# Six late heads of wo in place of four at the end of the load stream of a decode kernel

## The chip, the cores and the metric

One core of a Trainium2 chip. PE is its engine for matmuls (TensorE), DVE and ACT are the vector and the scalar engine, SyncE (SP in the views) issues the loads, and PSUM is the memory that the matmuls write. The granted clock is the share of PE's full clock that the records show. The time is that of one execution on the device, in microseconds, as a median over executions. The profiles are single executions; the span in a profile is shorter than the time of the same execution (652.63 against 654.05 for the kernel before), and a place in the trace counts from the start of the span.

## The reference

One decode step: attention of one query token over a KV cache of 8192 positions, then an output projection, gated by a small MLP. The cache is what costs: 4 batches x 8 KV heads x 8192 x 256 x 2 bytes, twice, is 268 MB of the 279 MB that the core reads.

```python
def _A_ref(x, k_cache, v_cache, wq, wo):      # x: (4, 1, 448), caches: (4, 8, 8192, 256)
    q = (x @ wq).reshape(B, Sq, 16, 256).transpose(0, 2, 1, 3)
    k, v = repeat(k_cache, 2, axis=1), repeat(v_cache, 2, axis=1)
    p = softmax(einsum("bhqd,bhkd->bhqk", q, k) * 256 ** -0.5)
    o = einsum("bhqk,bhkd->bhqd", p, v)
    return o.transpose(0, 2, 1, 3).reshape(B, Sq, 4096) @ wo     # wo: (4096, 448)

# xn = layernorm(x); the result is x + A(xn, ...) * silu(B(xn, ...)), B a small two-layer block
```

## The kernel before

There are 32 pairs of batch and KV head ("heads" 0 to 31 below). For each, PE transposes K by matmuls, DVE and ACT carry the transposes out of PSUM, PE makes the scores, and so on; V's product for a head is made while the next but one is at work. All large loads go through one queue, in the order in which SyncE issues them. The 16 query heads of `wo`, the weights of the output projection (229 KB each), are loaded in two parts: twelve at the front, behind the first two K loads, and four at the very end, behind the last pieces of V.

```python
    PIECES = (0, 32, 48, 56, NCH)          # the last V comes in four pieces
    LATE = ((0, 1), (2,), (3,))            # heads of wo that are loaded last: one load each group
    NLATE = sum(len(g) for g in LATE)
# ...
            load_k(0)
            load_k(1)
# ...
            load_wo(NLATE, HQ, "dwo")          # the early load of wo
            for h in range(2, NH):
                load_k(h)                      # waits until the K buffer of head h - 2 is free
                load_v(h - 2)                  # waits until the V buffer is free
            load_v(NH - 2)
            load_v(NH - 1)                     # four pieces
            for i, hs in enumerate(LATE):
                load_wo(hs[0], hs[-1] + 1, "dwl%d" % i)
```

After the last head, PE runs `finish`. It fills waits with products of heads of `wo` that are there already (`f_ou`) and with idle matmuls (`f_warm`), takes the last V piece by piece, and ends with the output products that need the late heads (`f_o`: four matmuls of 224 columns for a head).

```python
            def finish():
                f_bc(h)
                take(pe, "dwo", 16)
                f_ou(range(NLATE, HQ - 3 * REP))
                take(pe, "v_po")
                f_warm(4)
                take(pe, "a_exp")
                # ... four heads more of f_ou, products of V of head 30, then of the first pieces of 31
                f_direct(NPIECE - ND)
                take(pe, "v_po")
                # ... eight small matmuls (L775 of the profile)
                f_direct(NPIECE - 1).then_inc(S["p_pv"], 1)
                take(pe, "dwl0", 16)
                f_o(LATE[0])
                take(pe, "v_ot")
                f_o(range(HQ - REP, HQ))       # the two heads that need the last V
                for i in range(1, len(LATE)):
                    take(pe, "dwl%d" % i, 16)
                    ins = f_o(LATE[i], i == len(LATE) - 1)
                ins.then_inc(S["p_o"], 1)
```

DVE then multiplies by the gate and adds x, and the result is stored.

## Time and profile before

| | kernel before |
|---|---|
| time, median of 3 | 653.84 us (653.25 to 654.87) |
| bytes read, mean rate | 279 MB, 427 GB/s over the span |
| last K lands, first transpose of it | 617.39, 617.53 |
| last V piece lands, its first use | 646.59, 648.19 |
| last wo load lands | 648.82 |
| output matmuls | 648.79 to 650.31 |

From the page of the profile, the span in 40 slices: the clock that PE was granted in tenths, and the busy share of the 16 DMA engines in tenths; then the bytes read.

```profile
PEclk9977999898889987888888789988878997797989
DMA  9999999999999999999999999999999999999996
HBM read 278.99 MB, written 0.00 MB: 427 GB/s over the span
```

The load stream is full from the first slice to the last but one. A kernel like this can only end earlier if the stream ends earlier, or if less is left to do after it.

SyncE's issues at the end (start, duration, what), from the timeline of that engine, and for two of them the time from issue to landing from the view of the DMA issues:

```profile
590.31 0.33 SPq L251 DMA_DIRECT2D kn<-in_A_k_cache_dram  x1
616.47 1.85 SPq L266 DMA_DIRECT2D kn<-in_A_v_cache_dram  x4
620.60 8.43 SPq L276 DMA_DIRECT2D wo_sb<-in_A_wo_dram  x1
...
kn<-in_A_k_cache_dram SPq DMA_DIRECT2D x1, 4096.0 KB, 27.1
wo_sb<-in_A_wo_dram SPq DMA_DIRECT2D x1, 224.0 KB, 28.2
```

The last K was issued at 590.31 and landed 27.1 us later, at 617.4; the last wo load landed at 620.60 + 28.2 = 648.8. All landings in this text are read so, from the single issues.

PE at the end, from its timeline (start, duration, what):

```profile
646.72 0.57 PE L733 MATMUL pst<-pT,kn 128*128 128x32 bf16 x16
647.38 1.10 PE L775 MATMUL pst<-sel,po 128*128 128x32 f32 x8
648.31 0.56 PE L733 MATMUL pst<-pT,kn 128*128 128x32 bf16 x16
648.79 1.52 PE L723 MATMUL pst<-wo_sb,OT_all 128*32 128x224 bf16 x24
```

The 24 output matmuls are one row: no wait for a load inside. The last load landed at 648.82, when only the first two of them had started; the four that need it started at 649.9. The chain of work that ended last (start, duration, what) says the same, it goes back through PE's own work and not to a load:

```profile
647.38 1.10 PE pst L775 x8
648.47 0.39 PE pst L733 x16
648.87 1.46 PE pst L723 x24
650.33 0.02 issue
650.35 0.40 DVE res L559
```

And the clock in the last head: busy time by engine in one stretch (PE, PEld, DVE, ACT, POOL), then PE's granted clock, the DMA share and GB/s. Over most of this stretch the clock was halved; the records have it at half from 617.3 to 624.1.

```profile
617.00:624.50 7.50, 6.97 (x85) 6.79 (x86) 2.14 (x4) 3.16 (x7) 0.00 (x0) 0.54 0.99 428
```

### The profile page before, as it was taken

The page shows a single profiled execution, that of the slowest core. Times are in us where ns is not written, and L with a number is a line of the kernel's source. Part 1 is how long each engine was busy: PE and PEld are TensorE (multiplying, and loading weights), DVE is VectorE, ACT ScalarE, POOL GpSimd, SP SyncE. Part 2 cuts the span into 40 slices and gives each one's busy share as a digit, 9 for nine tenths or more (in the row PEclk, how much of TensorE's full clock was granted, in tenths as well). Part 3 has the DMA queues.
Part 4 walks back from the last instruction along what each step waited for, and adds up shares of the span by engine and source line. Part 5 has one row for each costly group of instructions (what it writes and reads, how often), then busy time and mean ns, then how long its engine had stood idle before and what let it go on. Part 6 is the DMA issues. An engine that isn't in the chain of part 4 may idle for free. (4 is left out here: it accounts for less than half of the span.)

```text
span 652.6 us, 22794 instructions
## 1 busy us (share of the span) xinstructions
PE 553.5 (85%) x9927; PEld 474.8 (73%) x9927; DVE 276.6 (42%) x622; ACT 256.2 (39%) x364; POOL 3.6 (1%) x17
## 2 busy tenths in 40 slices
PE   2889997987888988888998888898888898887898
PEld 1668886876667887766887676698767678775785
DVE  7433554443444443444444344444344444343442
ACT  3423553443324443433444233444333344342340
POOL 2000000000000000000000000000000000000000
PEclk9977999898889987888888789988878997797989
DMA  9999999999999999999999999999999999999996
GB/s 380 443 414 436 427 436 428 440 428 440 428 440 428 438 430 436 432 434 434 434 431 430 434 432 436 430 438 428 440 428 440 428 436 430 438 428 440 428 428 285
DMA packets 12497, 279.13 MB, mean 428 GB/s; under 512 B 1220, under 2 KB 3272, under 8 KB 3784
## 3 DMA queue, kind: packets, MB, share of 16 engines
q1 hardware_dynamic: 12472, 278.99, 99.4%
q8 instruction: 7, 0.11, 0.1%
q14 instruction: 2, 0.02, 0.0%
q10 hardware_dynamic: 16, 0.01, 0.0%
HBM read 278.99 MB, written 0.00 MB: 427 GB/s over the span
## 5 line engine op out<-in xcount | busy, mean ns | idle before, releaser
L624 PE MATMUL pst<-ident_b,kn 128*128 128x128 bf16 x4096 | 347.1, 239 | 78.2 <-PEq L294 77.1
L325 ACT ACTIVATE kT<-pst 128x1024 bf16<-128x1024 bf16 x224 | 229.5, 1025 | 359.3 <-ACTq L294 358.2
L624 PEld LDWEIGHTS pst<-ident_b,kn 128*128 128x128 bf16 x4096 | 276.0, 108 | 84.3 <-issue 83.7
L323 DVE COPY kT<-pst 128x1024 bf16<-128x1024 bf16 x288 | 197.6, 691 | 261.5 <-DVEq L294 261.5
L636 PE MATMUL psc<-qc,kT 128*128 128x2 bf16 x4096 | 178.3, 164 | 2.1 <-issue 2.1
L636 PEld LDWEIGHTS psc<-qc,kT 128*128 128x128 bf16 x4096 | 157.2, 98 | 31.4 <-issue 31.2
L675 PE MATMUL psv<-vb,pT 128*4 128x512 bf16 x1056 | 87.7, 384 | 0.0
L654 PE MATMUL psm<-sel,po 128*128 128x2 f32 x272 | 36.8, 257 | 0.5 <-PEq L294 0.5
L654 PEld LDWEIGHTS psm<-sel,po 128*128 128x128 f32 x272 | 34.8, 196 | 1.0 <-issue 1.0
L675 PEld LDWEIGHTS psv<-vb,pT 128*4 128x4 bf16 x1056 | 22.3, 82 | 14.9 <-issue 0.9
L483 DVE TENSOR_REDUCE rmax<-psc 128x2 f32<-128x128 f32 x32 | 9.3, 292 | 48.8 <-DVEq L294 48.8
L501 DVE COPY po<-psv 128x512 f32<-128x512 f32 x34 | 23.5, 691 | 3.0 <-DVEq L294 2.3
L488 DVE TENSOR_REDUCE gmax<-psm 2x1 f32<-2x128 f32 x32 | 8.9, 279 | 33.4 <-DVEq L294 33.4
L347 ACT ACTIVATE pT<-psc,negb 128x64 bf16<-128x64 f32 x66 | 20.7, 333 | 5.4 <-ACTq L294 5.4
L648 PEld LDWEIGHTS psm<-diag,ones_f 2*128 2x128 f32 x66 | 14.1, 264 | 6.4 <-issue 5.2
L648 PE MATMUL psm<-diag,ones_f 2*128 2x2 f32 x66 | 16.8, 322 | 1.0 <-PEq L294 0.9
L347 ACT ACTIVATION_READ_ACCUMULATOR pT<-psc,negb 128x1 f32 x66 | 13.6, 206 | 0.0
L644 PEld LDWEIGHTS psm<-ident_f,rmax 128*2 128x2 f32 x32 | 2.6, 80 | 14.4 <-issue 14.4
L666 PE MATMUL psm<-rowsum,ones_f 128*128 128x2 f32 x64 | 11.6, 251 | 0.0
L666 PEld LDWEIGHTS psm<-rowsum,ones_f 128*128 128x128 f32 x64 | 9.5, 188 | 0.0
L491 DVE TENSOR_SCALAR diag<-ident_f,gmax 2x2 f32<-2x2 f32 x32 | 6.9, 217 | 4.8 <-DVEq L294 1.4
L569 PE MATMUL pst<-ident_b,xn_b 4*128 4x4 bf16 x14 | 0.7, 163 | 9.6 <-DVE xn_b L395 9.6
(101 smaller groups left out, 98.7 us busy)
## 6 DMA issues: line engine op xcount, KB each, us to landing
kn<-in_A_k_cache_dram SPq DMA_DIRECT2D x31, 4096.0 KB, 25.5
vb<-in_A_v_cache_dram SPq DMA_DIRECT2D x31, 4096.0 KB, 31.1
kn<-in_A_k_cache_dram SPq DMA_DIRECT2D x2, 2048.0 KB, 24.6
vb<-in_A_wq_dram SPq DMA_DIRECT2D x1, 3584.0 KB, 11.1
vb<-in_B_w_dram SPq DMA_DIRECT2D x2, 1568.0 KB, 15.4
wo_sb<-in_A_wo_dram SPq DMA_DIRECT2D x1, 2688.0 KB, 42.5
kn<-in_A_v_cache_dram SPq DMA_DIRECT2D x1, 2048.0 KB, 25.1
kn<-in_A_v_cache_dram SPq DMA_DIRECT2D x1, 1024.0 KB, 27.1
```

The costliest lines, as they stand in the source:

```text
L323: engine.tensor_copy(dst, src).then_inc(S["v_ev"], 1)
L325: engine.activation(dst, src, ACT.Copy).then_inc(S["a_ev"], 1)
L347: ins = act.activation(pv_p[:, :, hh], sc[:, :, hh], ACT.Exp, bias=negb[:, s, hh:hh + 1], scale=SCALE, accum_out=rowsum[:, s, hh:hh + 1])
L483: v.tensor_reduce(rmax[:, :], psc[h % 2][:, 0:NCH * REP].rearrange("p (k h) -> p h k", h=REP), AX.X, ALU.max).then_inc(S["v_rmax"], 1)
L488: v.tensor_reduce(gmax[:, :], psm[0:REP, 0:P], AX.X, ALU.max).then_inc(S["v_s"], 1)
L501: v.tensor_copy(po[:, slot], psv[:, 0:CP * DH]).then_inc(S["v_po"], 1)
L624: ins = pe.transpose(dst[:, t * P:(t + 1) * P], kn[:, h % 2, GC * j + kl, half * P:(half + 1) * P], ident_b[:, :])
L636: ins = pe.matmul(psc[h % 2][:, kk * REP:(kk + 1) * REP], kT[:, j % RING, t * P:(t + 1) * P], qc[:, h % 2, half, :], start=(half == 0), st ...
L648: pe.matmul(psm[:, P:P + REP], ones_f[0:REP, :], diag[:, :], start=True, stop=True).then_inc(S["p_m2"], 1)
L654: ins = pe.matmul(dst(dh)[:, 0:width], po[:, slot, i * DH + dh:(i + 1) * DH:NHALF], sel[:, i, 0:width], start=(i == 0), stop=(i == CP - 1))
L666: pe.matmul(psm[:, P + REP:P + 2 * REP], ones_f[:, :], rowsum[:, h % 2, :], start=True, stop=True)
L675: ins = pe.matmul(psv[o:o + CP * REP, 0:CP * DH], pT[:, h % 2, kk * REP:(kk + CP) * REP], src[:, kk:kk + CP, :].rearrange("p c d -> p (c d)"),
```

## The change

The intent: two more heads of `wo` (459 KB) go from the early load to the end. All of K and V lands earlier by the time that those bytes take, and PE can finish the last head under the loads of `wo`. The late heads come in loads of two, two, one and one.

```diff
-    LATE = ((0, 1), (2,), (3,))
+    LATE = ((0, 1), (2, 3), (4,), (5,))
```

In the instruction order this takes four matmuls of 448 columns out of the first `f_ou` group (12 to 8) and adds eight of 224 columns to the last group (24 to 32). The early load has ten heads in place of twelve, and SyncE issues one load more. DVE, ACT and GpSimd are the same.

## The prediction

> **What bounds the kernel now.** Two things in turn. Almost everywhere it is the load stream: the 40-slice row shows the 16 DMA engines at nine tenths or more in every slice but the last, 428 GB/s over the span, 279 MB in one queue. No load is issued too late by the issue and landing times; tightest are the K load of head 3 (issued 61.28 us, the one before it landed 65.57) and that of head 2 (issued 40.18, the one before, wo, landed 46.23). PE waits for each K load: the last K (head 31) lands at 617.39 and its first transpose starts at 617.53.
>
> From there to the end it is no longer the stream but the chain of PE, DVE and ACT on the last head. Landings in the trace against use: V pieces land 641.62, 644.07, 645.35, 646.59 and are first used at 643.49, 645.12, 646.72, 648.19; late wo lands 647.70, 648.26, 648.82 and the 24 output matmuls run without a gap from 648.79 to 650.31. Every landing comes 1 to 2 us before its use. The chain of waits agrees: PE and DVE work, no DMA.
>
> **What the change does.** The bytes stay; two heads of wo (459 KB) move from the load behind the first two K loads to the end of the stream. The 12-head load took 6.66 us (39.57 to 46.23), so two heads take 1.11 us. Everything between, the last K and V pieces included, lands 1.11 us earlier; the last wo load still lands at about 648.8. One more DMA issue costs nothing: SP has 20 us to spare.
> PE: four matmuls of 128x448 leave the first group after the last head (about 0.75 us, but PE then waits for ACT's exponentials, so about 0.1 us of it counts), and eight of 32x224 join the last group, 55 ns apart by their starts: +0.44 us, on the critical path.
>
> **Sum.** -1.11 (last K earlier) +0.44 (eight more matmuls at the end) and 0 to -0.1 (shorter first group) = about -0.7 us on an execution like the profiled one. The last wo load would be used at about 649.4, still 0.6 us after landing.
>
> The gain depends on the state of the PE clock in the last head. In the profile the granted clock was half from 617.3 to 624.1 and that head took 17.3 us from first transpose to its row-maximum transpose; others took 14.6 with no half-clock stretch, 16.0 with 3.4 us of it. [...] its half-clock stretches are 3.4 or 6.8 us. So executions differ. Where the last head is fast, both kernels end on the last wo load at the same time and the gain is about zero. Average: -0.5 us.
>
> **Predicted time:** 653.3 us, range 652.4 to 654.1. Faster by over 2%: 0.5%; within 2%: 99%; slower by over 2%: 0.5%.
>
> **Right if:** the last K lands near 616.3, the last V piece near 645.5, the last wo load still near 648.8; 32 output matmuls end near 649.6 in one run without a gap; the chain of waits still ends in PE and DVE work.
>
> **Wrong if:** the shorter early wo load lets the queue run dry before the K load of head 2 or 3 (their margins fall to 5 and 3.2 us); small late loads run slower than 413 GB/s, so that a gap opens in the 32 matmuls; or the clock's phase hides a difference of 0.5 us.

## The result

653.59 us (653.26 to 654.64, 6 runs) against 653.56 (653.25 to 654.87, 6 runs). The ratio is 1.000, with a 95% interval of 0.9987 to 1.0013, that is 0.85 us either way.

The changed kernel's profile, in the same views. The slices and the bytes:

```profile
PEclk9997999897798979779987888998788988878999
DMA  9999999999999999999999999999999999999997
HBM read 278.99 MB, written 0.00 MB: 428 GB/s over the span
```

The issues at the end, and the time to landing of two:

```profile
591.90 0.33 SPq L251 DMA_DIRECT2D kn<-in_A_k_cache_dram  x1
614.77 1.85 SPq L266 DMA_DIRECT2D kn<-in_A_v_cache_dram  x4
634.76 3.60 SPq L276 DMA_DIRECT2D wo_sb<-in_A_wo_dram  x1
...
kn<-in_A_k_cache_dram SPq DMA_DIRECT2D x1, 4096.0 KB, 24.6
wo_sb<-in_A_wo_dram SPq DMA_DIRECT2D x1, 224.0 KB, 14.3
```

The last K landed at 616.48 (0.9 us earlier) and the last wo load at 649.04 (0.2 us later). PE's end:

```profile
645.92 0.56 PE L733 MATMUL pst<-pT,kn 128*128 128x32 bf16 x16
646.90 0.98 PE L723 MATMUL pst<-wo_sb,OT_all 128*32 128x224 bf16 x16 [0.43 <-PEq L294]
648.06 1.53 PE L723 MATMUL pst<-wo_sb,OT_all 128*32 128x224 bf16 x16 [0.17 <-PEq L294]
```

Now there are waits: before the first output matmul, between the two rows, and inside the second, where the starts of single matmuls jump from 648.78 to 649.18. Those are the landings of the four late loads (646.77, 647.92, 648.49, 649.04). The chain of work that ended last has no PE work left before the last four output matmuls:

```profile
649.18 0.42 PE pst L723 x4
649.60 0.02 issue
649.62 0.39 DVE res L559
650.02 0.02 issue
650.04 0.38 DVE out_b L561
```

So in this execution the last load decided the end, where in the profile before it was PE's chain. The clock differed as well: only 3.4 us at half in the last head.

```profile
617.00:624.50 7.50, 7.50 (x126) 7.38 (x123) 3.52 (x6) 4.68 (x8) 0.00 (x0) 0.77 1.01 437
```

The two profiles are thus one execution with a slow last head and one with a faster last head, and the time between the medians is nil. Two profiles can't tell whether the change or the clock made the difference.

### The profile page after: what moved, and what is told of

Its sections match the earlier page's. It is cut to its first block, busy times and chain, and to the rows that moved or that the text cites. A ratio compares the mean times of both kernels' runs of the same rounds, so it can differ in the third digit from the quotient of the medians.

```text
span 651.9 us, 22804 instructions
## 1 busy us (share of the span) xinstructions
PE 552.0 (85%) x9931; PEld 474.3 (73%) x9931; DVE 276.6 (42%) x622; ACT 256.0 (39%) x364; POOL 3.6 (1%) x17
## 5 line engine op out<-in xcount | busy, mean ns | idle before, releaser
L675 PE MATMUL psv<-vb,pT 128*4 128x512 bf16 x1056 | 86.1, 379 | 0.0
L648 PE MATMUL psm<-diag,ones_f 2*128 2x2 f32 x66 | 16.1, 310 | 1.1 <-PEq L294 0.9
L644 PEld LDWEIGHTS psm<-ident_f,rmax 128*2 128x2 f32 x32 | 2.6, 80 | 14.0 <-issue 14.0
```

Of the source, the lines that this page charges most:

```text
L648: pe.matmul(psm[:, P:P + REP], ones_f[0:REP, :], diag[:, :], start=True, stop=True).then_inc(S["p_m2"], 1)
L675: ins = pe.matmul(psv[o:o + CP * REP, 0:CP * DH], pT[:, h % 2, kk * REP:(kk + CP) * REP], src[:, kk:kk + CP, :].rearrange("p c d -> p (c d)"),
```

## The experiments

Theory A: the end is the later of two. One is the last wo load plus a fixed rest. The other is PE's chain, which starts when the last K lands and is longer when the clock is halved in the last head. The change moves the chain and not the last load, so it helps only executions in which the chain is the later one. Theory B: the chain gains in all executions, but the additional small loads end the stream later and take it back. Theory C: the shorter early load of `wo` gives it back, because the queue runs short before K of head 2 or 3, whose issue must wait for a buffer.

Twelve kernels ran, in three calls, each on one chip with its own runs of the kernel before: 653.77 us in the first call, 653.82 in the second, 653.50 in the third (medians of 11).

### Two late heads

```diff
-    LATE = ((0, 1), (2,), (3,))
+    LATE = ((0,), (1,))
```

> The opposite direction: two late heads (one and one) in place of four. Theory A (the kernel ends with the later of two things: the last wo load plus its few matmuls, or the PE chain that starts with the last K load): the last K lands 1.1 us later than in the kernel before, eight output matmuls fewer give 0.44 us back, so +0.2 us where the last head runs fast and +0.7 us where the clock is halved for long; median about 654.0 to 654.3, and in the profile the output matmuls follow the work before them without a gap while the last wo load has landed over 1 us before. Theory B (moving bytes to the end gains on the chain, but the extra small loads end the stream later and take it back): fewer late loads end the stream about 0.1 to 0.2 us earlier, time equal to the kernel before or lower.

654.86 us (654.13 to 655.42) against 653.77, ratio 1.0018 (1.0005 to 1.0031). The last K landed at 618.79, the last wo load at 649.09, where it is in the changed kernel too. So fewer late loads do not end the stream earlier, which speaks against theory B. The output matmuls ended at 650.37, 1.28 us after the last landing: chain-bound, although the last head was a faster one (16.0 us). The loss by the medians, 1.1 us, is above the 0.7 us that theory A gave at most, though the interval (0.3 to 2.0 us) includes that. In the profile the eight matmuls saved did not pay: from the last transpose of the last head's maxima to the end of the output matmuls it took 15.44 us, as in the kernel before. The longer first group took 0.20 us more, and with only four matmuls ahead of `v_ot`, PE's starts there were 0.38 us apart, against 0.19 before.

### Eight late heads

```diff
-    LATE = ((0, 1), (2,), (3,))
+    LATE = ((0, 1), (2, 3), (4, 5), (6,), (7,))
```

> Eight late heads (2, 2, 2, 1, 1). Theory A: the end is set by the last wo load, which lands at the same time as before within 0.2 us (648.8 to 649.1), so the time is that of four and of six late heads in a fast execution, about 653.3, and even the executions with the longest half-clock stretch no longer show, so that the spread shrinks to under 0.6 us. Gaps stand in the 40 output matmuls. Theory B: each further small load costs, so the last landing moves to 649.2 or later and the time goes up by 0.2 us or more against the changed kernel.

653.74 us (653.39 to 654.49) against 653.77, ratio 0.9998 (0.9985 to 1.0011). The end of PE, from its timeline:

```profile
646.98 2.44 PE L723 MATMUL pst<-wo_sb,OT_all 128*32 128x224 bf16 x36
649.58 0.41 PE L723 MATMUL pst<-wo_sb,OT_all 128*32 128x224 bf16 x4 [0.16 <-PEq L294]
```

The last four matmuls waited for the last load, although the clock was at half for 6.8 us in this last head and it took 17.3 us, as long as in the profile before. That is theory A: with eight late heads the slow clock no longer shows. But the spread did not shrink under 0.6 us as expected, and the last load landed at 649.44, 0.4 us late, as theory B had it. The place of the loss is not the end, though, and not the number of loads. From the last K to the last wo landing it took 30.29, 31.43, 32.57 and 33.69 us with two, four, six and eight late heads: 1.12 to 1.14 us for each two heads. With six heads in a single load (next experiment) it took 32.55 us, with six in four loads 32.57, so small loads cost the stream nothing that shows. The loss that the profile shows is at the front: the K loads of heads 2 and 3 took 10.15 and 10.10 us in place of 9.67. They were issued only 3.4 and 3.9 us before the load in front of them landed. That is what theory C expects, at a larger dose than in the change; but in two profiles below a load issued 4.0 us ahead lost nothing (9.67 us, the changed kernel with the fill) and one issued 4.6 us ahead lost 0.34 (10.01 us, the changed kernel again), so the lead alone does not decide it.

### Six late heads in one load

```diff
-    LATE = ((0, 1), (2,), (3,))
+    LATE = ((0, 1, 2, 3, 4, 5),)
-                f_o(range(HQ - REP, HQ))
+                ins = f_o(range(HQ - REP, HQ), len(LATE) == 1)
```

> Six late heads, but in one load, so that 24 of the 32 output matmuls have to wait for the last byte (the eight of the last pair of heads run before them or behind them). Theory A: +1.1 to +1.5 us against the changed kernel (20 to 28 more matmuls of 55 ns behind the last landing), about 654.7; this shows that the last landing is what the end hangs on. Theory B: three loads fewer, stream ends 0.2 us earlier or so, so +0.9 or less. If the time does not move, the last landing does not bound the end.

656.57 us (655.70 to 659.78), ratio to before 1.0047 (1.0028 to 1.0066): +2.8 us by the medians, twice the expectation. The direction is theory A's, the last landing (649.08) decides. In the profile 2.6 us of it lie between that landing and the end of the span (5.46 us, against 2.86 in the changed kernel), and 0.5 us outside the span, unexplained. Part of the 2.6 us has another cause, seen in PE's timeline and in the stretch of it:

```profile
649.22 3.00 PE L723 MATMUL pst<-wo_sb,OT_all 128*32 128x224 bf16 x32 [2.69 <-PEq L294]
...
649.20:652.30 3.10, 3.00 (x32) 2.79 (x32) 0.04 (x1) 0.00 (x0) 0.00 (x0) 0.57 0.00 0
```

PE stood still for 2.7 us before the load; in the records the clock was then halved from 648.5 to 651.9, and 32 matmuls took 3.0 us, 94 ns each, where 24 took 1.5 in the kernel before. So here loads in small steps were worth more than their matmuls: they also kept PE at work (in the profile of the changed kernel PE's longest wait there was 0.43 us, and the clock was full from 635 us on). The half-clock stretch lasted 3.4 us and began 1.9 us into the idle stretch of 2.7 us.

### Filling PE's wait for K

Twelve idle matmuls at the head of each head's work, in the kernel before and in the changed one.

```diff
+            def f_fill(h, n):
+                ptf = pT[:, :, :].rearrange("p s n -> p (s n)")
+                for i in range(n):
+                    pe.matmul(psc[h % 2][0:PVW, 0:ptf.shape[1]],
+                              pT[:, h % 2, NCH * REP:NCH * REP + PVW], ptf, start=True, stop=True)
             def body(h):
+                f_fill(h, 12)
```

> The kernel before with 12 idle matmuls (320 columns, about 0.14 us each, result overwritten) at the head of each head's work, where PE waits about 2 us for K. Theory A with the clock as the cause of the slow executions: the clock is no longer halved in the last head (granted clock near 1.0 over the span), that head takes about 14.6 us in place of 16 to 17.3, and all executions end on the last wo load, about 653.2, spread under 0.6 us; the kernel before gains 0.3 us and its slow executions (654.9) vanish. If the clock stays as it was, the cause of the spread is not shown by this run. If the clock is full and the spread stays, the clock was not its cause.

> The changed kernel with the same 12 idle matmuls at the head of each head's work as in the run with the kernel before (653.33 us there, span 651.9, last head 14.6 us). Theory A (later of last landing and PE chain; in fast executions the last landing decides in both kernels): 653.3 us, the same as the kernel before with the fill within 0.2 us, the output matmuls with gaps, last landing 649.0. Theory C (the shorter wo load at the front leaves the queue too little work, so that the K load of head 2 or 3 is issued late and starts with a loss): K of head 2 is issued under 3 us before the load in front of it lands, its own load takes 10.1 us or more in place of 9.67, everything after it lands later by as much, and the time is 653.7 or more.

Kernel before with fill: 653.33 us (653.24 to 653.94), ratio 0.9993 (0.9981 to 1.0006). Changed kernel with fill: 653.48 us (653.21 to 653.65), ratio 0.9991 (0.9978 to 1.0004). The last head took 14.59 us in both profiles. In the kernel before with fill, the stretch of the last head has the full clock, and PE's output matmuls now come 0.75 us sooner, behind a wait:

```profile
617.00:624.50 7.50, 6.75 (x132) 6.67 (x133) 3.52 (x6) 4.57 (x8) 0.00 (x0) 1.00 0.97 419
...
648.04 1.56 PE L731 MATMUL pst<-wo_sb,OT_all 128*32 128x224 bf16 x24 [0.42 <-PEq L294]
```

So the clock in the last head made the chain late, and without that the kernel before is bound by its last load too, as theory A says. Two marks of the expectation were missed: the mean clock was 0.958 and not near 1.0, and the spread 0.70 us in place of under 0.6. Theory C got little support at this dose: in the changed kernel with the fill, the K load of head 2 was issued 4.0 us ahead and took 9.67 us, as usual, and that of head 3, issued 5.0 us ahead, took 9.91, 0.24 us too long.

The fixed rest can be read from all profiles. From the landing of the last wo load to the end of the span it took 2.86 or 2.87 us in the changed kernel (two profiles), with eight late heads, in both filled kernels and in the kernel with an early load of only four heads further down, all with a wait before the last output matmuls. In the kernel before it took 3.81 us, with two late heads 3.59, with the front half of the change alone (two heads in mid-stream) 3.37, all without such a wait. That is the mark of the two regimes, where four matmuls follow the last load: 2.87 us is the floor, what is above it is the chain.

An estimate from these profiles tells where the two ends cross. In the kernel before, the first transpose starts 0.14 us after the last K, the last head follows, and then 15.44 us to the end of the output matmuls; by the other way the last load lands 31.43 us after the last K, and the four last matmuls end 0.55 us later. The two are equal for a last head of 16.4 us. In the changed kernel (32.57 us, and a chain 0.18 us longer, see below) it is 17.4 us. In the profiles of both kernels, heads with 3.4 us of half clock took 16.0 to 16.1 us, those with 6.5 or 6.6 us 17.3 to 17.4. So the kernel before is bound by its chain only when clearly more than 3.4 us of its last head run at half clock, and the changed kernel hardly ever. The same sum gives 0.73 and 0.51 us above the floor for the profiles with two late heads and with the front half alone; measured were 0.72 and 0.50.

### A longer chain, by PE

To see the chain's own gain in the time, 20 idle matmuls went into `finish` of both filled kernels.

```diff
                 f_ou(range(NLATE, HQ - 3 * REP))
+                f_warm(20)
```

> The kernel before with the fill and 20 idle matmuls (448 columns, about 3.7 us) in the PE chain right after the last head. Both kernels must now be bound by the chain and the clock is full, so that the chain's own gain is seen without the rest. Theory A: chain end of the filled kernel without stream waits 647.8 plus 3.6, so output matmuls end at about 651.4 in place of 649.6, time about 655.1. No gaps in the 24 output matmuls.

> The changed kernel with the fill and the same 20 idle matmuls. Theory A: 0.5 to 0.8 us faster than the kernel before with fill and delay (1.11 us from the earlier K load, 0.44 us given back by eight more output matmuls), about 654.4; no gaps in the 32 output matmuls or only at the last load. If the two are equal, the chain itself did not gain and theory A is wrong. If theory C holds too, the last K lands less than 1.11 us earlier.

660.45 us (660.14 to 661.02) and 657.14 us (656.45 to 659.93), ratios to before 1.0101 (1.0086 to 1.0116) and 1.0057 (1.0039 to 1.0075). That is 5.3 us and 2.7 us more than expected, so these times can't be used for the chain. The cause is in mid-kernel, where the outer loop begins its second round and the inner loop's code is needed again after a jump over the `finish` code. First, for the kernel before with fill and delay, the instruction packets on the page (number, MB, share) and PE's wait before the first idle matmul (L685) near that place, from the waits (us in total, times, longest); then the same two for the kernel before with the fill alone:

```profile
q8 instruction: 16, 0.26, 0.2%
...
PE psc L685 <- issue: 14.9, 1, 14.9
```

```profile
q8 instruction: 7, 0.11, 0.1%
...
PE psc L685 <- issue: 0.7, 1, 0.7
```

Nine more packets of 16 KB and a standstill of 15 us: the stream ran short, and the last K landed at 621.11, in place of 617.61. Eight of the nine came between 330 and 385 us in both profiles. Why the longer code brought them was not tried.

What the two profiles do show is the chain, since neither had a wait for a load in its output matmuls. First before, then changed (the transpose of the maxima, L644, and the output matmuls):

```profile
637.20 0.27 PE L644 MATMUL psm<-ident_f,rmax 128*2 128x128 f32 x1
654.91 1.52 PE L731 MATMUL pst<-wo_sb,OT_all 128*32 128x224 bf16 x24
...
633.82 0.27 PE L644 MATMUL psm<-ident_f,rmax 128*2 128x128 f32 x1
651.33 1.90 PE L731 MATMUL pst<-wo_sb,OT_all 128*32 128x224 bf16 x32
```

From the last transpose of the last head's maxima to the end of the last output matmul it took 19.24 us before and 19.42 after: 0.20 less up to the first output matmul, 0.38 more in the 32. So the chain is 0.18 us longer, and by the distance from the last K to the last landing (31.43 and 32.57 us) it starts 1.1 us earlier.

### A longer chain, by DVE

The second attempt left PE's code alone and put a useless reduction into DVE's part.

```diff
+            c(v.tensor_reduce(rmax[:, 0:1], kT[:, 6:8].rearrange("p s n -> p (s n)"), AX.X, ALU.max))
+            c.sync()
             f_negb(h)
```

> The kernel before with one useless DVE reduction (128x2048, estimated from its 2048 columns to take about 2.2 us) in the chain after the last head; PE's code is unchanged, other than in the pair with 20 idle matmuls, where longer PE code brought nine more instruction loads and a stall of 14 us in mid-kernel. The chain is now the later one in every execution. Theory A: chain end goes from about 649.0 to 650.3 (3.4 or 6.8 us of half clock in the last head) up by 2.2 us, time 655.0 to 656.5, median about 655.5, no gaps in the output matmuls, last wo load landed 2 us earlier.

> The changed kernel with the same DVE reduction. Theory A: where the chain decides, the change gains what was worked out from the profiles: 1.1 us (last K earlier) less 0.2 to 0.45 us (chain longer by eight output matmuls, shorter by the first group), so 0.65 to 0.95 us under the kernel before with the same delay, about 654.7. Rival (the chain did not gain, or the front gives it back): equal within 0.3 us.

659.08 us (655.58 to 659.55) and 658.36 us (657.29 to 659.24), ratios to before 1.0078 (1.0063 to 1.0092) and 1.0074 (1.0061 to 1.0087). The medians differ by 0.7 us in the direction of theory A, the ratios by 0.0004, 0.3 us, with intervals that overlap almost wholly: inconclusive. The reduction took 2.28 us as wanted, but it made PE wait (2.4 us in one place in the profile of the changed kernel), and in the profile of the changed kernel the clock was halved for 6.8 us from 637.9, inside `finish`. Two stretches, first of the kernel before with the delay, then of the changed one (columns as above, the granted clock is the third number from the right):

```profile
634.00:642.00 8.00, 4.96 (x65) 3.52 (x66) 3.87 (x7) 0.70 (x4) 0.00 (x0) 1.00 0.93 397
```

```profile
634.00:642.00 8.00, 5.62 (x50) 3.61 (x47) 2.76 (x5) 0.70 (x4) 0.00 (x0) 0.75 0.95 402
```

The profiled execution of the first was its fastest (655.58 us), with the full clock in `finish`, in the expected range. Four of the other five took 658.8 to 659.6. That the clock was halved in those is a guess; none was profiled.

### The changed kernel again

No edit.

> The changed kernel unaltered, for more executions and a second profile. Theory A: median 653.5, lowest 653.2 to 653.4 as for the kernel before, and in the profile gaps in the output matmuls whatever the clock did in the last head; the granted clock of the last head does not decide the time. Theory C: in the slower executions a K load of head 2 or 3 takes over 10 us.

653.38 us (653.27 to 655.42, 6 runs) against 653.82, ratio 0.9996 (0.9983 to 1.0010). A second profile with waits before the last loads and 2.86 us from the last landing to the end. The K load of head 2, issued 4.6 us ahead, took 10.01 us in it, but the last K landed at 616.45 all the same, as in the first profile. One execution took 655.42 us and was not profiled, so it is open what made it slow.

### The front half of the change alone

Late loads as in the kernel before, and two of the early heads (then eight of them) moved to mid-stream, so that only the front gets shorter.

```diff
-            load_wo(NLATE, HQ, "dwo")
+            load_wo(6, HQ, "dwo")            # 12 in the second kernel
             for h in range(2, NH):
                 load_k(h)
                 load_v(h - 2)
+                if h == 20:
+                    load_wo(4, 6, "dwm")     # 4 to 12 in the second kernel
# finish waits for "dwm" behind "dwo"
```

> Only the front half of the change: late loads as in the kernel before (four heads), the early wo load cut to ten heads, and heads 4 and 5 loaded in mid-stream. The order at the end is that of the kernel before, the last K should land at the same time (617.4). Theory A: time of the kernel before within 0.3 us. Theory C (the cut early load makes K loads of head 2 or 3 late): the last K lands 0.3 to 1 us later in the profile, a K load of head 2 or 3 takes over 9.9 us, time up by 0.3 to 1 us, as the kernel before has a chain that follows the last K.

> The front half at four times the dose: early wo load of four heads, eight heads in mid-stream, late loads as in the kernel before. The early load now ends at about 41.8 us, 1.6 us after K of head 2 is issued at 40.2 at the earliest. Theory C (the early wo load is filler for the queue): a loss of 1 to 3 us at the K loads of head 2 and 3, last K at 618.4 to 620.4, time up by 1 to 3 us. If the loss is under 0.3 us, the filler is not needed and the front of the change is free.

With two heads: 653.55 us (653.34 to 654.11) against 653.50, ratio 0.9997 (0.9984 to 1.0010). The K loads of heads 2 and 3 took 9.67 and 9.69 us. The last K did land 0.5 us later than in the kernel before (617.89), as theory C had it, but not by those loads: the V load that landed at 336.13 took 10.30 us. In all profiles but that of the kernel before, one load that lands in mid-kernel (327 to 340 us) takes 9.76 us or more in place of 9.67, and an instruction packet falls near its time (324 to 329 us), where PE's outer loop begins its second round; the cause was not tried. So at the dose of the change the front costs nothing that this can see. With eight heads: 655.97 us (655.17 to 658.14), ratio 1.0040 (1.0027 to 1.0054), and the last K at 620.11. The stretch from 40 to 42 us, first in the kernel before, then in this one (columns as above):

```profile
40.00:42.00 2.00, 2.00 (x36) 0.90 (x32) 0.80 (x2) 0.00 (x0) 0.00 (x0) 0.60 1.05 406
```

```profile
40.00:42.00 2.00, 2.00 (x40) 1.13 (x39) 1.04 (x2) 0.00 (x0) 0.00 (x0) 0.74 0.91 261
```

The last number is the rate, 406 and 261 GB/s: the K load of head 2 was issued at 40.42, when only 1.2 us of the early wo load were left, and took 12.47 us. So the early wo load is the filler that keeps the stream full until the first K buffer is free. Theory C is right about the mechanism, but it does not show in the time of this change, which leaves 5.9 and 4.6 us of filler at that load in its two profiles (9.67 and 10.01 us for the load).

## Why the prediction was right or wrong

- **What bounds the kernel.** Right for the execution that was profiled: chain-bound, 0.94 us above the floor (3.81 less 2.87). Too wide as a statement on the kernel: of the 39 executions of the kernel before, 18 took under 653.6 us, near the 653.3 of the filled kernel, and 13 over 654.
- **The last K 1.11 us earlier, the last wo load where it was.** Right. From the last K to the last landing it is 1.14 us more. The last K landed 0.9 us earlier and the last wo load 0.2 us later in the first profile, where the V load in mid-kernel took 9.95 us, 0.28 too long; kernels with four late heads had their last landing between 648.80 and 649.33, those with six between 648.74 and 649.23 (kernels with PE delays or eight heads in mid-stream left out), so that 0.2 us is within the scatter of single executions.
- **The chain 0.34 to 0.44 us longer.** Somewhat too long: +0.38 for the eight matmuls, -0.20 for the shorter first group, sum +0.18 (the pair with 20 idle matmuls).
- **"The last wo load would be used at about 649.4, still 0.6 us after landing."** This did not hold in any profile of the changed kernel. With a faster last head the last four matmuls started at 649.18 and waited for it. That the matmuls ended at 649.59, with 649.6 predicted, is a coincidence: a different term decided.
- **"Average: -0.5 us."** This is the step that the runs do not bear out. It took the profiled execution for the usual one, where its own text says that a fast last head leaves nothing to gain; by the crossing at 16.4 us, a head of 16.0 us leaves nothing either. Measured: ratios of 1.000 and 0.9996, each with about 0.9 us either way. The two medians of the changed kernel lie 0.03 us above and 0.44 us below those of before. A gain of 0.5 us is not excluded and not shown: 8 of 12 executions of the changed kernel took under 653.6 us, against 18 of 39, which points to a gain and is too few. The time, 653.59 us, lies in the range, but so does the 653.56 of the kernel before, so that this says little.
- **Where the gain went.** Off the critical path: in both profiles of the changed kernel, PE is ready early and stands before the last loads, and the end is the last landing plus 2.87 us, which the change does not touch. The loss to small loads at the end (theory B) was not found (32.55 us with one load, 32.57 with four), and a loss at the front (theory C) shows only from a larger dose.
- **What stays open.** Three of twelve executions of the changed kernel took over 654 us, one 655.42. The last head's clock should not make that much difference any longer, as the profile with eight late heads showed, and no such execution was profiled. Two candidates are untried: a halved clock in `finish`, as in the profile with the DVE delay, and a larger loss of the stream in mid-kernel. In the kernel before, the four slowest of the 33 executions with a clock on record (654.76 to 655.42 us) have the four lowest mean clocks (0.882 to 0.888, the others 0.890 and more); that points to the clock there, but the changed kernel's 655.42 us had 0.898. The filled kernels had none over 654 in ten executions; that is too few, and neither filled kernel is clearly faster than the kernel before.

## What to carry to other kernels

A profile is one execution: before you value a change of the tail, find out which of two ends decides, and in how many executions, by a mark that is the same in all profiles (here the time from the last landing to the end, 2.87 us when the load decides). When the load stream is full to the end, as here, reordering it gains only what the compute chain stood behind the last load (0.94 us in the profile of the kernel before), and not a bit more: eight late heads gave a ratio of 0.9998. Small, useful loads at the front may be the filler that keeps the queue busy while buffers are not yet free, so check the time between an issue and the landing in front of it before taking bytes away there (with eight heads taken away, 1.2 us of it were left and the next load took 12.47 us in place of 9.67).

## What the traces show of the clock, the instruction packets and a load's lead

- A halving of the clock came 1.9 us into an idle stretch of 2.7 us (six late heads in one load), and another 1.9 us into the wait of 2.2 us before the last head's transposes (kernel before). Stretches of 3.4 and 6.8 us at half were usual in a kernel that keeps PE busy 85% of the span: 27 in the profile of the kernel before, 24 in that of the changed one. The last head took 14.6, 16.0 or 17.3 us with none, 3.4 or 6.8 us of it, and that much decided which of two ends came last.
- Twenty more matmuls in code that is jumped over brought nine more instruction packets of 16 KB and a standstill of PE of 14 to 15 us at one loop boundary (14.9 and 13.9 us in the two profiles).
- A load issued 1.2 us before the load in front of it landed took 2.8 us more than usual (12.47 us in place of 9.67, 4 MB); leads of 3.4 and 3.9 us cost about 0.45 us each in one profile, 4.0 us cost nothing in another and 4.6 us cost 0.34 us in a third, so the lead alone does not decide it.
